# One of eight sums made by a ScalarE copy and an adding transfer instead of VectorE, from the fourth unit on

## The chip, the core and the metric

The kernel runs on one core of a Trainium2 chip. The core has five engines that work beside each other, each in its own program order, and wait for each other through semaphores: TensorE (PE for its products, PEld for loading their weights), VectorE (DVE), ScalarE (ACT), GpSimd (POOL) and SyncE (SP), which only issues transfers. ScalarE and GpSimd can issue transfers too. The metric is the device time of one execution in microseconds (us); lower is better.

## The reference

Two stages. The first is a recurrent attention over 4 batches, 8 heads, 768 positions and 48 columns a head:

```
state = 0                                         # per batch and head, 48 x 48
for t in range(768):
    y[t]  = r[t] @ (state + (u * k[t]) outer v[t])
    state = w[t][:, None] * state + k[t] outer v[t]
```

The second takes y as x, 3072 rows (batch and position) of 384 columns, through two layers, all in float32:

```
h = x @ w_in                    # 384 -> 2048
g = h * (1 / (1 + exp(-h)))
out = g @ w_out                 # 2048 -> 384
```

The change touches what is made of g ahead of the last product.

## The kernel before

The work is cut into 12 units. A unit is 128 positions of two batches, so 256 rows of x; units 0 to 11 go through the batches' halves, then on to the next 128 positions. The first units differ from the rest; from unit 3 on (`NFAST = 3`) everything named below is alike.

**Rounds.** The loop of line 1442 runs over i = 3 to 11. In round i three units are in work: the attention of unit i (the groups that `mix(i)` lists, lines 965 to 1071), the first layer of unit i - 1 (`ups`, 20 steps) and the second layer of unit i - 2 (`downs`, 7 steps). The seven steps of `downs` come first and the 20 of `ups` behind them; the groups are laid between them, each with a count of steps that follow it. After round 11 come the second layer of unit 10, the first layer of unit 11 and the second of unit 11, with no attention beside them: the tail. The order of every engine's program is the order in which these lines are reached; each engine keeps to it, and no planner moves anything.

**First layer.** Each of the 20 steps of `ups` is one `first_part(i, n)`: eight products of 64 columns of weights on TensorE into one of four banks, and then a copy, a sum or the activation that the step owes. The 20 steps stand for the layer's block products; sums of weights and of x take the place of some blocks. The results, g, are eight tiles of 128 partitions by 512 columns, named `gt[i, x, b, m]`: x the lower or upper half of the 2048 columns, b the batch, m which half of that half. Step 17 makes `gt[i, 1, 0, 0]`, step 18 and step 19 make tiles of m = 1.

**Sums for the second layer.** The second layer is computed with seven products of blocks instead of eight (line 1322), and four of these take sums of g's blocks on their left. `sums(i, m)` (line 1293) makes the four for one half m, into `quarters`, a part of the tile `temps`:

```
s1 = lower[1] + upper[1]     s3 = lower[0] - lower[1]
s2 = s1 - lower[0]           s4 = upper[0] - s2
```

in this order, each 128x512, at line 1306 on VectorE. `sums(i, 0)` stands behind step 17, `sums(i, 1)` behind step 19. (Unit 3 makes two of its m = 1 sums a round later.) So eight sums a unit, four for each m.

**Second layer.** The seven products run in the order of `downs`: the first two take g itself, the third s2, the fourth s1, the fifth s3, the sixth s4, the seventh g again. Each takes the eight tiles f of one kind, the four of m = 0 first. They add into three banks in the order x, z, x, y, x, y, x (`place`, line 1326). After the second, fifth and sixth, VectorE adds the bank to a part that ScalarE has copied out (line 1343); after the others ScalarE copies it (line 1340). So the seventh product, which adds to bank x, has to wait until VectorE has read bank x after the fifth.

**What stands around the sums in a round.** Ahead of step 17, VectorE writes into the scores (`block_write`, L573). Behind it GpSimd has `bonus_steps(i + 1, 1, 2, 3)`, four multiplications at L497 (in round 4 step 0 of it and a product as well, in round 5 seven products of `tw` at L414 stand ahead of step 17). Then come steps 18 and 19 and the last group: the attention's output on TensorE, copied by ScalarE (`kq` L831, `yt` L873), VectorE's transposes of the next unit's `tk` (L365), which GpSimd's next work (L655) reads, and the update of the state. The next round starts with the second layer's first products, VectorE's transposes of `tr`, its work on the queries (L628, L783) and on sums of x (L1152 to L1172), among which the L1343 after the fifth product has its fixed place.

**Transfers.** SP issues nearly all: loads of the next units in small pieces, the way of y through device memory to x (`turned<-yt`, `xt<-turned`), the output. ScalarE issues a few in the first units. GpSimd issues none.

## Time and profile before

| | us |
|---|---|
| median of three runs | 566.93 (566.53 to 567.62) |
| the profiled execution | 567.41 |
| its span, first instruction to last | 565.6 |
| busy: TensorE products, weights | 555.8, 517.6 |
| busy: VectorE, GpSimd, ScalarE | 477.0, 395.7, 274.5 |
| VectorE's sums at L1306, 128x512, s1 and s3 of both m | 36 of 0.985 on average |

The profile is that of one execution, 0.48 us above the median of the runs. Lines L... are those of the kernel's file; where several places call one helper, all have its line. An instruction of the timeline shows its start, its length, engine, line, operation, what it writes <- what it reads, shapes, how many were merged into the row, and in brackets the idle time ahead of it with what ended it. GpSimd's spans are rough. The steady rounds take 42.4 us each from the start of one second layer to that of the next (298.68, 341.12, 383.55 in the chain of work that ended last), and the last two 41.1.

### The profile page before, as it was taken

The numbers are of one execution on the slowest core, as the hardware profiler recorded it, in microseconds if no ns is written. First come the engines' busy times: TensorE is split into PE (matmuls) and PEld (weight loads), VectorE is DVE, ScalarE is ACT, GpSimd is POOL, SyncE is SP. The second block draws the span as 40 slices with busy tenths as digits, with TensorE's granted clock in tenths as the row PEclk, the third lists the DMA queues.
The fourth block names the chain that finished last, engine by engine and source line by source line (L and its number), as shares of the span: only waits on it lengthen the run. The fifth ranks groups of instructions, "written<-read, shape, count | busy, mean of one in ns | idle before, by whom it ended". The sixth has DMA issues, their size and how long they took to land.

```text
span 565.6 us, 18886 instructions
## 1 busy us (share of the span) xinstructions
PE 555.8 (98%) x7782; PEld 517.6 (92%) x7782; DVE 477.0 (84%) x744; ACT 274.5 (49%) x620; POOL 395.7 (70%) x447
## 2 busy tenths in 40 slices
PE   8989999999999999999999999999999999999997
PEld 8767786699889999999999999999999999999997
DVE  7979788998999989999889989989989989882250
ACT  5679696362371373373374274274274272371330
POOL 5998988617879998969796696696696696700000
PEclk9999999999999999999999999999999999999999
DMA  9956876345345365365565554555555462102000
GB/s 224 314 104 191 213 213 133 49 69 115 99 76 99 80 105 94 59 131 95 104 104 93 113 93 89 108 96 94 111 88 95 99 102 65 38 5 57 29 9 21
DMA packets 206485, 57.59 MB, mean 102 GB/s; under 512 B 186048, under 2 KB 198208, under 8 KB 206400
## 3 DMA queue, kind: packets, MB, share of 16 engines
q1 hardware_dynamic: 203712, 54.23, 46.9%
q10 hardware_dynamic: 2688, 2.16, 1.6%
q8 instruction: 61, 1.00, 0.8%
q14 instruction: 24, 0.20, 0.1%
HBM read 47.14 MB, written 9.18 MB: 100 GB/s over the span
## 4 chain that ended last, share of the span: by engine, by line
PE 78%; DVE 8%; POOL 7%; DMA 3%; issue 2%; ACT 1%; SPq 0%; POOLq 0%; DVEq 0%
PE p_o L1335 24%; PE p_o L1191 14%; PE p_h L1191 9%; PE p_h L1084 8%; PE p_h L1335 4%; PE p_m L1273 4%; PE p_sc L704 3%; PE p_m L868 2%; PE p_sc L1335 2%; POOL tk L646 2%; POOL w_in_sb L260 2%; PE p_m L847 1%; DVE tr L628 1%; PE p_m L704 1%; POOL tw L414 1%
## 5 line engine op out<-in xcount | busy, mean ns | idle before, releaser
L646 POOL TENSOR_TENSOR tk<-tk,tw 128x256 f32<-128x256 f32 x112 | 91.7, 839 | 7.6 <-DVE tw L414 3.4
L1335 PE MATMUL p_o<-own,temps 128*128 128x192 f32 x496 | 82.9, 326 | 0.0
L1335 PEld LDWEIGHTS p_o<-own,temps 128*128 128x128 f32 x496 | 80.8, 190 | 0.3 <-DVE temps L1306 0.2
L1191 PE MATMUL p_o<-xt,w_in_sb 128*64 128x128 f32 x1152 | 72.5, 273 | 0.1
L414 POOL TENSOR_TENSOR tw<-tw 128x256 f32<-128x256 f32 (+6 forms) x71 | 42.3, 596 | 38.0 <-DVE tw L365 34.5
L1084 PE MATMUL p_h<-xt,w_in_sb 128*128 128x256 f32 x288 | 66.1, 384 | 1.8 <-POOL w_in_sb L260 1.6
L1191 PEld LDWEIGHTS p_o<-xt,w_in_sb 128*64 128x64 f32 x1152 | 64.9, 137 | 0.4 <-issue 0.4
L1084 PEld LDWEIGHTS p_h<-xt,w_in_sb 128*128 128x128 f32 x288 | 53.6, 190 | 10.0 <-POOL w_in_sb L260 2.4
L497 POOL TENSOR_TENSOR ruk<-tokens_rk 128x384 f32<-128x384 f32 x48 | 53.6, 1137 | 8.1 <-DMA tokens_rk<-in_k_dram 8.1
L1335 PE MATMUL p_o<-w_out_sb,gt 128*128 128x192 f32 x308 | 54.5, 330 | 0.4 <-DVE ob L1343 0.3
L628 DVE TENSOR_TENSOR tr<-tr,tw 128x512 f32<-128x512 f32 x57 | 51.9, 911 | 1.0 <-PE p_m L704 0.4
L1335 PEld LDWEIGHTS p_o<-w_out_sb,gt 128*128 128x128 f32 x308 | 50.0, 190 | 1.5 <-DVE ob L1343 0.9
L655 POOL TENSOR_TENSOR tk<-tk,tw 128x256 f32<-128x256 f32 x32 | 25.1, 812 | 27.5 <-DVE tk L365 27.5
L1306 DVE TENSOR_TENSOR temps<-gt 128x512 f32<-128x512 f32 (+1 forms) x48 | 42.9, 931 | 0.0
L1340 ACT COPY partial<-p_o 128x192 f32<-128x192 f32 x31 | 9.9, 319 | 66.6 <-PE p_o L1335 61.5
L616 ACT COPY tk<-tk 128x256 f32<-128x256 f32 x52 | 20.9, 402 | 37.2 <-POOL tk L646 27.4
L1215 ACT ACTIVATE gt<-p_o 128x512 f32<-128x512 f32 x45 | 26.0, 601 | 25.0 <-PE p_o L1191 25.0
L1335 PE MATMUL p_o<-w_out_sb,temps 128*128 128x192 f32 x176 | 30.5, 326 | 0.0
L722 DVE COPY_PREDICATED score<-mask,p_sc 128x512 f32<-128x512 int8 x38 | 28.4, 807 | 1.4 <-PE p_sc L704 1.3
L1335 PE MATMUL p_h<-w_out_sb,gt 128*128 128x192 f32 x168 | 29.1, 326 | 0.0
L1335 PEld LDWEIGHTS p_o<-w_out_sb,temps 128*128 128x128 f32 x176 | 28.9, 190 | 0.1
L497 POOL TENSOR_TENSOR spare<-tokens_rk 128x384 f32<-128x384 f32 x24 | 28.5, 1198 | 0.6
(251 smaller groups left out, 1314.0 us busy)
## 6 DMA issues: line engine op xcount, KB each, us to landing
w_out_sb<-in_moe_w_in_dram SPq DMA_DIRECT2D x6, 768.0 KB, 7.4
turned<-yt SPq DMA_DIRECT2D x18, 192.0 KB, 2.7
xt<-turned SPq DMA_DIRECT2D x9, 384.0 KB, 3.3
w_out_sb<-in_moe_w_out_dram SPq DMA_DIRECT2D x4, 768.0 KB, 7.4
own<-in_moe_w_out_dram SPq DMA_DIRECT2D x4, 768.0 KB, 4.7
tokens_w<-in_w_dram SPq DMA_DIRECT2D x8, 384.0 KB, 4.5
tokens_rk<-in_r_dram SPq DMA_DIRECT2D x7, 384.0 KB, 4.4
tokens_rk<-in_k_dram SPq DMA_DIRECT2D x7, 384.0 KB, 5.8
```

What stands on the lines that cost most here:

```text
L414: engine.tensor_tensor(out=up, in0=t[:, :, 0::2], in1=t[:, :, 1::2], op=ALU.mult)
L497: mul = lambda out, one, two: nc.gpsimd.tensor_tensor(out=out, in0=one, in1=two, op=ALU.mult)
L628: nc.vector.tensor_tensor(out=odd, in0=odd, in1=tw[i][l][:, :, 0::2][:, :, :, None].to_broadcast([128, Q, L >> (l + 1), c]), op=ALU.mult)
L646: nc.gpsimd.tensor_tensor(out=out, in0=have, in1=odd_products(i, l, b, *blocks), op=ALU.mult)
L655: nc.gpsimd.tensor_tensor(out=have, in0=have, in1=odd_products(i, l, b, [2, NP * ni]), op=ALU.mult)
L704: nc.tensor.matmul(to, lhsT=tk[i][rows, X[l % 2] + p, x * 64:(x + 1) * 64], rhs=have, start=True, stop=True)
L722: nc.vector.copy_predicated(out=dst, mask=masks[l][:, :, None].to_broadcast([128, NB, NP, ni, c]), data=sc[e].rearrange("p (b q) (i c) -> ...
L1084: nc.tensor.matmul(p_h[:, a, :], lhsT=w_in_sb[:, c, f * 128:(f + 1) * 128], rhs=xt[i][:, c, :], start=(a == 0 and c == 0), stop=(a == 1 an ...
L1191: nc.tensor.matmul(p[h:h + PD, q, :], lhsT=left[:, f:f + PD], rhs=right, start=first and q == 0, stop=q == 3, skip_group_check=True)
L1215: nc.scalar.activation(out=g(f, t), in_=have, func=AF.Silu)
L1306: nc.vector.tensor_tensor(out=out, in0=one, in1=two, op=op)
L1335: nc.tensor.matmul(p, lhsT=left(f), rhs=right[:, f, :], start=which in (0, 1, 3) and f == 0, stop=f == FH - 1, skip_group_check=True)
```

## The change

From unit 3 on, and for m = 0 alone, s1 is no longer made by VectorE. ScalarE copies `lower[1]` into the place of s1, and a transfer issued by GpSimd adds `upper[1]` to it there (`accum_op`). The other seven sums of a unit stay on VectorE; s2 reads what the transfer leaves. The four sums of m = 0 are also split over two steps: s1 and s3 stay behind step 17, s2 and s4 go behind step 18. In units 1 and 2 nothing changes, and no sum has another value.

```diff
@@ def sums(i, m, which=range(4)):
         made = ((s1, lower[1], upper[1], ALU.add), (s3, lower[0], lower[1], ALU.subtract),
                 (s2, s1, lower[0], ALU.subtract), (s4, upper[0], s2, ALU.subtract))
-        for out, one, two, op in (made[x] for x in which):
-            nc.vector.tensor_tensor(out=out, in0=one, in1=two, op=op)
+        for x in which:
+            out, one, two, op = made[x]
+            if x == 0 and i >= NFAST and m == 0:
+                nc.scalar.copy(out=out, in_=one)
+                nc.gpsimd.dma_start(out=out, in_=two, accum_op=ALU.add)
+            else:
+                nc.vector.tensor_tensor(out=out, in0=one, in1=two, op=op)
@@ def ups(i):
             made = [[(first_part, i, n)] for n in ORDER]
             if i == len(units) - 1:
                 made[10].append((sums_of_x, i, 7))
-            made[17].append((sums, i, 0))
+            made[17].append((sums, i, 0, (0, 1)))
+            made[18].append((sums, i, 0, (2, 3)))
             made[-1].append((sums, i, 1, range(4) if i > NFAST else (0, 2)))
             return made
```

## The prediction

> **What bounds the kernel now.** I read the page's busy shares first, then its forty slices.

> ```profile
> PE 555.8 (98%) x7782; PEld 517.6 (92%) x7782; DVE 477.0 (84%) x744; ACT 274.5 (49%) x620; POOL 395.7 (70%) x447
> ...
> DVE  7979788998999989999889989989989989882250
> ```

> TensorE is busy for 98% of the span, VectorE nearly always until the last four slices, ScalarE half the time. So the change eases an engine that is full but is not the bound: it gains only where TensorE waits for VectorE, and loses wherever VectorE or GpSimd becomes late for TensorE. Next, the list of waits, for what little TensorE waits for:

> ```profile
> PEld p_sc L704 <- POOL tk L646: 2.3, 9, 0.5
> ...
> PEld p_o L1335 <- DVE ob L1343: 0.9, 2, 0.6
> ```

> Total us, times, longest us: small (the next such line, of L1191 behind L1218, has 0.8), but they name the tight places. L1335 behind L1343 is the seventh product of a unit's second layer (I call it Q7; line 1334): it adds to the bank "x" that VectorE's sum after the fifth product must have read. So I read the end of a steady round, round 7, and the start of round 8 in the timeline, engine by engine:

> ```profile
> 336.95 2.89 DVE L1306 TENSOR_TENSOR temps<-gt 128x512 f32<-128x512 f32 x2
> 339.77 1.50 DVE L1306 TENSOR_TENSOR temps<-temps,gt 128x512 f32<-128x512 f32 x1
> 341.37 0.69 DVE L1306 TENSOR_TENSOR temps<-gt,temps 128x512 f32<-128x512 f32 x1
> ...
> 344.51 1.30 DVE L365 STREAM_TRANSPOSE tk<-raw 128x512 f32<-128x512 f32 x2
> ...
> 356.12 0.36 DVE L1343 TENSOR_TENSOR ob<-p_o,partial 128x192 f32<-128x192 f32 x1
> ...
> 334.87 3.00 POOL L497 TENSOR_TENSOR ruk<-ruk,u_bc 128x384 f32<-128x384 f32 x2
> 337.84 1.46 POOL L497 TENSOR_TENSOR spare<-tokens_rk 128x384 f32<-128x384 f32 x1
> 339.37 1.34 POOL L497 TENSOR_TENSOR tokens_rk<-tokens_rk,tokens_w 128x384 f32<-128x384 f32 x1
> 345.30 3.04 POOL L655 TENSOR_TENSOR tk<-tk,tw 128x256 f32<-128x256 f32 x4 [4.58 <-DVE tk L365]
> ...
> 336.36 1.09 ACT L1215 ACTIVATE gt<-p_h 128x512 f32<-128x512 f32 x2
> ...
> 356.59 2.63 PEld L1335 LDWEIGHTS p_o<-w_out_sb,gt 128*128 128x128 f32 x16
> ```

> Columns: start and length in us. Three things to see. VectorE runs without an idle time from the sums of L1306 to the sum of L1343, which ends at 356.48, and Q7's first weights load at 356.59: 0.11 us of slack (the same in rounds 7, 9 and 10; in round 11, 481.76 against 482.55, 0.8). A sum of L1306 takes 0.69 us (every 0.61) while GpSimd is idle, and 1.5 (every 1.42) while GpSimd multiplies at L497; those multiplications, 1.0 each alone, take 1.3 to 1.5. And GpSimd starts these four at 334.87, before the sums.

> **The change, part by part.**

> *Removed:* nine sums s1 on VectorE (units 3 to 11): 1.42 us in a steady round.

> *Added on ScalarE:* nine copies of 128x512. The nearest row is ScalarE's copy of L785, the same shape, 0.61 at 329.53. The copy stands behind the activation that feeds the fourth sum, second of the pair at 336.36, which ends at 337.45; so it ends at 338.0. What is behind it on ScalarE moves by 0.6: two activations, two copies of kq that end at 339.2, then copies of yt that have 0.6 us of idle time ahead of them. The update's products read kq at 340.2. Cost nothing; without that idle time up to 0.6 a round.

> *Added on GpSimd's queue:* the transfer, which must wait for the copy. GpSimd gets there at 334.87, and it works in order, so the four multiplications of L497 wait until 338.0 plus what issuing takes. No row shows a transfer issued by GpSimd. Bounds for the issue: 0 (the engine goes on at once) and 2.0 (two multiplications of L497); I take 1.0, one multiplication. They then run from 339.0. They were followed by 4.6 us of idle time, so GpSimd's own end costs nothing; what counts is that they now meet other sums.

> *Added, issue to landing:* 256 KB within on-chip memory. Rows: 64 KB to `kept` 1.6, 192 KB `turned<-yt` 2.7, 384 KB `xt<-turned` 3.3, 384 KB `tokens_rk<-in_k_dram` 6.9 on ScalarE's queue. I take 3.5, just above the third, since the bytes it adds to are read too; ends 1.6 and 6.9. [...]

> *The new wait:* s2 reads s1, so VectorE stops until 338.0 + 3.5 = 341.5, after finishing s3 near 337. Behind s2 stand s4, the four sums of the other half, the transposes of tk and tr, the queries and x sums of the next round, and L1343. Cost in a steady round: by 341.5 GpSimd has done 2.5 multiplications; 1.5 remain and meet sums. From the landing to the transposes: 1.5 x 1.42 + 4.5 x 0.61 = 4.9, so 346.4 against 344.51: **VectorE is 1.9 late**, although a sum fewer. This hardly depends on my two unknowns: a sooner landing only meets more multiplications. Landing in 1.6 with free issue gives 339.65 + 2.4 x 1.42 + 3.6 x 0.61 = 345.2, 0.7 late. At 6.9 and 2.0: 344.9 + 6 x 0.61 = 348.6, 4.1 late.

> *Where it reaches TensorE:* nothing idles on VectorE until L1343, so Q7 waits 1.9 − 0.11 = 1.8. The products that read the sums do not feel it: the second uses of s2 end near 345.8, and are read from 347.6. The bursts of scores have over 4 us.

> *Moved:* s2 and s4 go one step later in the program, behind the four multiplications (another engine's) and a first-layer step. On VectorE nothing lies between; cost nothing, since the transfer is later anyway.

> *Sum.* Rounds 6 to 9 (paid at Q7 of rounds 7 to 10): 4 x 1.8 = 7.2. Round 10 (paid in 11): 1.9 − 0.8 = 1.1. Two earlier rounds differ:

> ```profile
> 250.17 6.18 POOL L414 TENSOR_TENSOR tw<-tw 128x512 f32<-128x512 f32 x7
> ...
> 259.64 1.29 DVE L365 STREAM_TRANSPOSE tk<-raw 128x512 f32<-128x512 f32 x2
> ```

> Round 4: the activation ends at 209.4, the copy at 210.0, landing 213.5; GpSimd has over seven operations then, so all four sums behind meet them: 213.5 + 4 x 1.42 = 219.2, against transposes at 217.66 in the timeline: 1.5 late; Q7 already waits for VectorE there (0.56), so 1.5 in full. Round 5: seven products hold GpSimd until 256.3, so the transfer starts only then, or from 255 if the quieter VectorE lets them run faster; landing 259.2 on the mean, + 4.9 = 264.1 against 259.64: 4.4 late, and Q7 waits there already (0.38): 4.4. Rounds 11 and the tail: GpSimd is empty; in the tail the copy ends at 543.9, landing 547.4, the second s2 ends at 550.5 and is read from 550.7: nothing.

> Total 7.2 + 1.1 + 1.5 + 4.4 = 14.2. The profiled execution took 567.41 (span 565.6), so 581.6; it lies 0.48 above the median of the runs, 566.93, so **581.1**. Low ends: 4 x 0.6 + 0 for round 11 + 0 for round 4 (all four sums from 211.6 end before 217.66) + 2.6 for round 5 = 5.0: 572. High ends: 4 x 4.0 + 3.3 + 3.3 + 5.9, and 3 in the tail = 31.5: 598.

> **The rivals.**

> *Faster: VectorE is relieved.* Slices of 9 speak for it. Decides if s2 needs no wait, and GpSimd's postponed multiplications fall beside the transposes, not the sums: without them the six sums take 3.7, so the landing must come before 340.8, under 2.8 after the copy. The gain is bounded by TensorE's waits for VectorE after 180 us, 0.9 + 0.8 (L1191 behind L1218), and for GpSimd's tk, which follows VectorE, 1.2 of the 2.3; I take half, 1.5: 565.4. Against it: the multiplications must go somewhere, and even a free landing at 338.0 gives 338.0 + 4 x 1.42 + 2 x 0.61 = 344.9, 0.4 late. [...]

> *No change: the lateness is absorbed.* The chain from the sums to L1343 would have to give back 1.9 us in 12; VectorE shows no idle time there. Needs a Q7 wait that the trace misnames. 567.

> *Worse: the transfer is the slow thing.* An adding transfer of 7 us gives the 598 above, and each further us costs one in eight places (rounds 4 to 10 and the tail): 614 at 9 us. Transfers of small pieces run beside it (DMA share 0.49 from 334 to 345), for it; 256 KB in rows of 2 KB, against.

> **How the numbers follow.** Forecast (VectorE late at Q7) 0.80, for 572 to 592: its ends are 572 and 598, and landings past 6 us are unlikely beside the rows of 2.7 and 3.3; slow transfer 0.07; faster 0.08; no change 0.05. The range 572 to 592 leaves out the other three, 0.2. Within 0.2% is 1.1 us either way, about what runs of this kernel can tell apart: faster 0.08, same 0.05, slower 0.87.

> **What would show it.** Right: idle time on VectorE ahead of L1306 in every unit from the fourth, ended by a transfer; L497 starting about 4 us later in its round; PEld L1335 waiting for L1343 some 14 us in all, most in round 6. Wrong: L1343 no later against Q7, sums of 0.69 throughout, or TensorE waiting at L1335 for the sums themselves.

## The result, and the profile after

The changed kernel takes 586.67 us (median; 585.5 to 590.31) against 567.27 of the kernel before: 1.0354 times as long, 95% interval 1.0335 to 1.0374. The forecast was 581.1 us in a range of 572 to 592, slower with a chance of 0.87. The profiled execution took 587.73 us (span 585.7), 20.3 more than that of before. In the new file the copy is line 1308, the transfer 1309, VectorE's sums 1311, the second layer's products 1340, ScalarE's copies of its banks 1345 and VectorE's sums of them 1348.

From the page of the changed kernel: busy shares, the granted clock in forty slices, the chain's shares by engine, and two groups (busy us, mean ns; then idle us ahead of them and what ended most of it).

```profile
PE 560.7 (96%) x7782; PEld 519.8 (89%) x7782; DVE 458.2 (78%) x735; ACT 279.0 (48%) x629; POOL 390.6 (67%) x456
...
PEclk9999999999999999999899999999999999999999
...
PE 57%; DVE 18%; issue 11%; DMA 5%; SPq 3%; POOL 3%; ACT 3%; DVEq 0%; POOLq 0%
...
L1311 DVE TENSOR_TENSOR temps<-temps,gt 128x512 f32<-128x512 f32 (+1 forms) x25 | 21.9, 877 | 46.2 <-DMA temps<-gt 46.1
...
L1309 POOL DMA_DIRECT2D temps<-gt x9 | 8.0, 886 | 63.5 <-ACT temps L1308 60.7
```

VectorE is busy 18.8 us less than before (477.0), more than the 9 × 1.42 = 12.8 of the sums taken away: those left are shorter too, and so are the writes into the scores (L573, 24.0 us against 27.0), as they meet fewer of GpSimd's multiplications (in round 7 the second of them took 1.92 us beside L497 before, and 1.33 with GpSimd idle now). But it stands still for 46 us behind the transfer, which was not there before, and TensorE fell from 98% of the span to 96%. Its 7782 products are the same; that they take 4.9 us more, and the slice whose clock reads 8, is the first sign (TensorE's granted clock in these traces is 1.0, full, or 0.5, half; the slice is a mean of both) of something that the prediction had no term for.

The waits of the changed kernel (total us, times, longest us) say where that standing still arrives, and the list of transfers gives the median from issue to landing:

```profile
DVE temps L1311 <- DMA temps<-gt: 46.1, 9, 6.4
PEld p_o L1340 <- DVE ob L1348: 14.9, 7, 3.5
...
```

```profile
temps<-gt POOLq DMA_DIRECT2D x9, 256.0 KB, 4.0
```

TensorE's wait at the seventh product of the second layer (Q7) has grown from 0.9 us to 14.9. The steady round that the prediction worked through, round 7, now looks like this in the timeline of the changed kernel, engine by engine (start, length in us; in brackets the idle time before and what ended it):

```profile
346.70 0.68 DVE L1311 TENSOR_TENSOR temps<-gt 128x512 f32<-128x512 f32 x1
353.78 0.69 DVE L1311 TENSOR_TENSOR temps<-temps,gt 128x512 f32<-128x512 f32 x1 [6.41 <-DMA temps<-gt]
...
357.72 1.30 DVE L365 STREAM_TRANSPOSE tk<-raw 128x512 f32<-128x512 f32 x2
...
348.58 0.87 POOL L1309 DMA_DIRECT2D temps<-gt  x1 [3.33 <-ACT temps L1308]
349.18 2.28 POOL L497 TENSOR_TENSOR ruk<-ruk,u_bc 128x384 f32<-128x384 f32 x2
...
352.49 1.01 POOL L497 TENSOR_TENSOR tokens_rk<-tokens_rk,tokens_w 128x384 f32<-128x384 f32 x1
...
347.67 0.62 ACT L1308 COPY temps<-gt 128x512 f32<-128x512 f32 x1
...
369.71 1.44 PEld L1340 LDWEIGHTS p_o<-w_out_sb,gt 128*128 128x128 f32 x9 [2.76 <-DVE ob L1348]
```

Up to here the changed kernel has lost 10.33 us (351.38 against 341.05 at the start of the next second layer), so subtract that to compare with the times in the prediction. Read from the top: VectorE makes s3 and then has nothing for 6.41 us; ScalarE's copy ends at 348.29; GpSimd, idle for 3.33 us, issues 0.3 us later; the data lands at 353.76, 5.17 us after the issue began. By then GpSimd has done its four multiplications (353.50), so the six sums run unhindered (353.78 to 357.72). The transposes start at 357.72 − 10.33 = 347.39 in the time of before, against 344.51: 2.9 us late, and Q7 waits 2.76.

What each round lost, from the starts of the second layers of the two profiled executions (worked out, start after minus start before, less the same of the round before):

| lost in round | 5 | 6 | 7 | 8 | 9 | 10 | 11 | tail |
|---|---|---|---|---|---|---|---|---|
| forecast, us | 1.5 | 4.4 | 1.8 | 1.8 | 1.8 | 1.8 | 1.1 | 0 |
| measured, us | 2.39 | 6.52 | 1.86 | 2.73 | 2.30 | 2.29 | 1.61 | 0.87 |

The tail is counted to the end of the span; up to the start of the last second layer it lost nothing. Together these are 20.6; the spans differ by 20.1, as the changed kernel was 0.43 us ahead where this count begins.

### The profile page after: what moved, and what is told of

It reads as the page before. It is cut to its first block, busy times and chain, and to the rows that moved or that the text cites. A ratio compares the mean times of both kernels' runs of the same rounds, so it can differ in the third digit from the quotient of the medians.

```text
span 585.7 us, 18908 instructions
## 1 busy us (share of the span) xinstructions
PE 560.7 (96%) x7782; PEld 519.8 (89%) x7782; DVE 458.2 (78%) x735; ACT 279.0 (48%) x629; POOL 390.6 (67%) x456
## 4 chain that ended last, share of the span: by engine, by line
PE 57%; DVE 18%; issue 11%; DMA 5%; SPq 3%; POOL 3%; ACT 3%; DVEq 0%; POOLq 0%
PE p_o L1340 13%; PE p_o L1191 11%; PE p_h L1084 8%; PE p_h L1191 8%; PE p_m L1273 4%; DVE tr L628 3%; SPq L127 3%; PE p_sc L704 3%; DVE temps L1311 2%; DVE block_sums L534 2%; DMA temps<-gt 2%; DVE score L722 2%; PE p_m L868 1%; PE p_m L847 1%; PE p_m L704 1%
## 5 line engine op out<-in xcount | busy, mean ns | idle before, releaser
L646 POOL TENSOR_TENSOR tk<-tk,tw 128x256 f32<-128x256 f32 x112 | 92.2, 843 | 8.0 <-DVE tw L414 3.8
L1191 PE MATMUL p_o<-xt,w_in_sb 128*64 128x128 f32 x1152 | 72.1, 273 | 0.0
L1340 PE MATMUL p_o<-w_out_sb,gt 128*128 128x192 f32 x308 | 57.6, 342 | 12.8 <-DVE ob L1348 12.8
L414 POOL TENSOR_TENSOR tw<-tw 128x256 f32<-128x256 f32 (+6 forms) x71 | 40.8, 574 | 40.9 <-DVE tw L365 37.4
L1340 PEld LDWEIGHTS p_o<-w_out_sb,gt 128*128 128x128 f32 x308 | 52.2, 197 | 15.5 <-DVE ob L1348 14.9
L1191 PEld LDWEIGHTS p_o<-xt,w_in_sb 128*64 128x64 f32 x1152 | 64.7, 137 | 0.1
L497 POOL TENSOR_TENSOR ruk<-tokens_rk 128x384 f32<-128x384 f32 x48 | 52.9, 1131 | 7.9 <-DMA tokens_rk<-in_k_dram 7.9
L1311 DVE TENSOR_TENSOR temps<-temps,gt 128x512 f32<-128x512 f32 (+1 forms) x25 | 21.9, 877 | 46.2 <-DMA temps<-gt 46.1
L1309 POOL DMA_DIRECT2D temps<-gt x9 | 8.0, 886 | 63.5 <-ACT temps L1308 60.7
L616 ACT COPY tk<-tk 128x256 f32<-128x256 f32 x52 | 20.9, 402 | 59.8 <-POOL tk L646 39.7
L655 POOL TENSOR_TENSOR tk<-tk,tw 128x256 f32<-128x256 f32 x32 | 24.6, 800 | 31.7 <-DVE tk L365 31.7
L1345 ACT COPY partial<-p_o 128x192 f32<-128x192 f32 x31 | 9.9, 318 | 59.9 <-PE p_o L1340 59.8
L1215 ACT ACTIVATE gt<-p_o 128x512 f32<-128x512 f32 x45 | 25.9, 601 | 24.7 <-PE p_o L1191 24.7
```

Source lines behind the costliest of these rows:

```text
L414: engine.tensor_tensor(out=up, in0=t[:, :, 0::2], in1=t[:, :, 1::2], op=ALU.mult)
L497: mul = lambda out, one, two: nc.gpsimd.tensor_tensor(out=out, in0=one, in1=two, op=ALU.mult)
L646: nc.gpsimd.tensor_tensor(out=out, in0=have, in1=odd_products(i, l, b, *blocks), op=ALU.mult)
L655: nc.gpsimd.tensor_tensor(out=have, in0=have, in1=odd_products(i, l, b, [2, NP * ni]), op=ALU.mult)
L1191: nc.tensor.matmul(p[h:h + PD, q, :], lhsT=left[:, f:f + PD], rhs=right, start=first and q == 0, stop=q == 3, skip_group_check=True)
L1215: nc.scalar.activation(out=g(f, t), in_=have, func=AF.Silu)
```

## The experiments

The theory: VectorE takes its work in order, so it is late by whatever the transfer's landing makes it late, and TensorE pays at the place without slack, Q7. GpSimd, in order too, is held until the copy ends, so its multiplications fall on VectorE's later sums. The rivals were other places for the cost: the split of the steps, the landing alone, the meetings alone, the issue on GpSimd. Runs of one group share runs of the kernel before: 566.96 us for the first four, 567.13 for the last four.

### The split alone

```
 for x in which:
     out, one, two, op = made[x]
-    if x == 0 and i >= NFAST and m == 0:
-        nc.scalar.copy(out=out, in_=one)
-        nc.gpsimd.dma_start(out=out, in_=two, accum_op=ALU.add)
-    else:
-        nc.vector.tensor_tensor(out=out, in0=one, in1=two, op=op)
+    nc.vector.tensor_tensor(out=out, in0=one, in1=two, op=op)
```

> The copy and the transfer are undone: s1 is VectorE's again in every unit. Only the split stays (s1 and s3 behind step 17, s2 and s4 behind step 18). Theory (the cost is VectorE's wait for the transfer): VectorE's order is unchanged, so 567 us within 1, and the seventh product waits for VectorE as before (0.9 us in all). Rival (placing s2 and s4 a step later costs by itself): 570 or more.

Measured: 567.27 us, ratio 1.0005 (0.9996 to 1.0015). The move of s2 and s4 by a step costs nothing that can be measured; the whole loss lies in the copy and the transfer.

### The copy kept, an add on GpSimd in place of the transfer

```
 nc.scalar.copy(out=out, in_=one)
-nc.gpsimd.dma_start(out=out, in_=two, accum_op=ALU.add)
+nc.gpsimd.tensor_tensor(out=out, in0=out, in1=two, op=op)
```

> ScalarE's copy stays; instead of the transfer GpSimd adds upper[1] in place with one 128x512 sum, in the same place of its queue. Theory A (what I predicted: GpSimd held behind the copy, and its four multiplications then meeting VectorE's sums): the sum is there 1.6 us after the copy, but s2 and the three sums behind it take 1.42 each, so VectorE is 2.0 late in rounds 6 to 10, 4.9 in round 5, and the time is 580 to 584. Theory B (the landing alone is the cost, meetings cost little): s2 is no later than before in rounds 6 to 10, 1.6 late in round 5: 568 to 570.

Measured: 581.72 us, ratio 1.0258 (1.0243 to 1.0273). Rounds 7 to 10 lose 1.65 or 1.66 each. The timeline of this kernel in a steady round, VectorE and then GpSimd:

```profile
303.55 1.48 DVE L1311 TENSOR_TENSOR temps<-temps,gt 128x512 f32<-128x512 f32 x1 [2.32 <-POOL temps L1309]
305.13 1.30 DVE L1311 TENSOR_TENSOR temps<-gt,temps 128x512 f32<-128x512 f32 x1
306.36 2.91 DVE L1311 TENSOR_TENSOR temps<-gt 128x512 f32<-128x512 f32 x2
...
310.51 1.30 DVE L365 STREAM_TRANSPOSE tk<-raw 128x512 f32<-128x512 f32 x2
```

```profile
302.25 1.27 POOL L1309 TENSOR_TENSOR temps<-temps,gt 128x512 f32<-128x512 f32 x1 [3.12 <-ACT temps L1308]
303.48 2.41 POOL L497 TENSOR_TENSOR ruk<-ruk,u_bc 128x384 f32<-128x384 f32 x2
```

Here s1 is ready 1.27 us after the copy, far sooner than any transfer, and the loss stays three quarters of the whole: four sums meet four multiplications. From 303.55 to 310.51 are 6.96 us, which is 4 × 1.42 + 2 × 0.61 = 6.9. So the two causes stand in for each other: an earlier landing buys meetings, as the prediction had it. The copy's end is what both hang on.

### The same copy and transfer, earlier

Both inputs of s1 are there some steps before. Here the copy and the transfer stand behind step 15 of the unit instead of step 17.

```
+if i >= NFAST and tuple(which) == (0,):        # the whole step: copy, then transfer
+    s1 = quarters[:, 0, 4 * m:4 * m + 4, :]
+    nc.scalar.copy(out=s1, in_=gt[i, 0, 1, m][:, :, :])
+    nc.gpsimd.dma_start(out=s1, in_=gt[i, 1, 1, m][:, :, :], accum_op=ALU.add)
+    return
...
-made[17].append((sums, i, 0, (0, 1)))
+made[15].append((sums, i, 0, (0,)))
+made[17].append((sums, i, 0, (1,)))
```

> Copy and transfer are issued behind step 15, as soon as lower[1] exists, two steps earlier. Both theories have the transfer issued near 335.2 of a steady round instead of 338.4 and landed by 339.2, when VectorE took up s2 in the kernel before (339.8). Theory (the wait for the landing is the cost, and an earlier place takes it away): 567 to 569, no wait of VectorE for the transfer over 2.5 us, the seventh product's wait for VectorE under 3 us in all. Rival (the copy on ScalarE or the transfer beside others costs wherever it stands): 573 or more.

Measured: 567.54 us, ratio 1.0005 (0.9983 to 1.0027). From the waits of this kernel, and its timeline in the round of before's 336.95:

```profile
DVE temps L1317 <- DMA temps<-gt: 13.0, 9, 3.1
...
PEld p_o L1346 <- DVE ob L1354: 0.9, 3, 0.4
```

```profile
338.10 0.69 DVE L1317 TENSOR_TENSOR temps<-temps,gt 128x512 f32<-128x512 f32 x1 [0.74 <-DMA temps<-gt]
...
343.49 1.30 DVE L365 STREAM_TRANSPOSE tk<-raw 128x512 f32<-128x512 f32 x2
...
334.67 0.87 POOL L1298 DMA_DIRECT2D temps<-gt  x1 [0.22 <-issue]
335.27 2.95 POOL L497 TENSOR_TENSOR ruk<-ruk,u_bc 128x384 f32<-128x384 f32 x2
```

GpSimd waits 0.22 us instead of 3.33 and VectorE 0.74 instead of 6.41; Q7 is back at 0.9 in all. One part of the expectation was missed: the longest wait of VectorE for the transfer is 3.1 us, not under 2.5, at 297.81, behind a transfer that took 5.75; TensorE did not feel it. The whole loss in the rounds is gone with the operations unchanged, so it was the place, not the price, of the copy and the transfer. And nothing is gained: VectorE starts its transposes 0.6 us earlier than before (343.49 against 344.51, in an execution that ran 0.46 us ahead at this place), and no place of TensorE can use it. That answers the first rival of the prediction: relief for VectorE, when it does come, is worth nothing measurable here.

### Unit 4 left on VectorE

```
-if x == 0 and i >= NFAST and m == 0:
+if x == 0 and i >= NFAST and i != 4 and m == 0:
```

> The change for all units from 3 on but unit 4, whose transfer is held up behind seven products on GpSimd and pays in round 6. Round 6 took 6.5 us longer in the changed kernel: 3.5 of wait at the seventh product, 1.3 at the third, and some 2.5 in which the granted clock of TensorE stood at 0.5 behind that wait. Theory (the clock falls because TensorE stood still there for 3.5 us): all 6.5 go, 580 to 581.5, the granted clock stays at 1.0. Rival (the clock falls for another reason, such as the new transfers as a whole): only 4 go, 582.5 to 584, and a stretch of 0.5 shows up elsewhere.

Measured: 581.95 us, ratio 1.0273 (1.0248 to 1.0298). Round 6 lost 0.12 instead of 6.52, so that round's loss was unit 4's transfer. But round 8 lost 4.10 instead of 2.73, in a stretch of TensorE at half clock (3.41 us from 363.04) that round 8 of the changed kernel had not shown. So the time fell between the two ranges expected, above the 581.5 of the theory: the round's loss went, as the theory had it, and half clock turned up elsewhere, as the rival had it. The rival's reason, the new transfers as a whole, is not needed for that: why half clock came there is told below, with the clock.

### The other half's sums first

s2 and s4 of the first half moved behind the four sums of the second, so that the landing has something to hide behind.

```
-made[18].append((sums, i, 0, (2, 3)))
 made[-1].append((sums, i, 1, range(4) if i > NFAST else (0, 2)))
+made[-1].append((sums, i, 0, (2, 3)))
```

> Copy and transfer as in the changed kernel; s2 and s4 of m = 0 go behind the four sums of m = 1 in VectorE's order, so that these run while the transfer is on its way. If waiting for the landing is the whole cost, the transfer is covered in rounds 6 to 10 and only round 5 (transfer held behind seven products) stays late: 568 to 570. If the postponed multiplications of GpSimd cost wherever they meet sums (theory), the four sums of m = 1 meet them from 339: 339.0 + 4 x 1.42 + 2 x 0.61 = 345.9, 1.4 late in each of rounds 6 to 10, 2.5 in round 5, nothing in round 4: 573 to 576.

Measured: 582.26 us, ratio 1.0263 (1.0244 to 1.0283). Both numbers missed: the steady rounds still lose 1.97 to 2.00 each, though VectorE now waits for the transfer in one unit of nine only, 0.8 us. From the timeline of this kernel, VectorE and GpSimd:

```profile
344.49 5.07 DVE L1311 TENSOR_TENSOR temps<-gt 128x512 f32<-128x512 f32 x2 [1.96 <-ACT gt L1215]
349.49 0.68 DVE L1311 TENSOR_TENSOR temps<-temps,gt 128x512 f32<-128x512 f32 x1
...
352.14 1.30 DVE L365 STREAM_TRANSPOSE tk<-raw 128x512 f32<-128x512 f32 x2
```

```profile
343.77 0.88 POOL L1309 DMA_DIRECT2D temps<-gt  x1 [3.34 <-ACT temps L1308]
344.37 2.27 POOL L497 TENSOR_TENSOR ruk<-ruk,u_bc 128x384 f32<-128x384 f32 x2
346.30 1.29 POOL L497 TENSOR_TENSOR spare<-tokens_rk 128x384 f32<-128x384 f32 x1
```

Two things took the landing's place. The second half's sums wait 1.96 us for ScalarE's activations, 0.6 of which is the copy ahead of them. And the first of those sums lasts 3.65 us (344.49 to 348.14; 0.69 alone), while GpSimd's first three multiplications run at 1.3 each beside it; the second takes 1.49. So VectorE lost the landing's wait and paid with another wait and a harder meeting. I had priced each meeting at 1.42, the measure of rows in which sums and multiplications alternate; here a sum arrived at a run of multiplications under way, and that price was too low. In each of the seven units 3 to 9 one sum lasted 3.65 to 5.70 us.

### The transfer behind the four multiplications

GpSimd's multiplications first, as before the change, and the transfer issued after them.

```
+if i >= NFAST and m == 0 and tuple(which) == (2, 3):
+    nc.gpsimd.dma_start(out=quarters[:, 0, 0:4, :], in_=gt[i, 1, 1, 0][:, :, :], accum_op=ALU.add)
...
 nc.scalar.copy(out=out, in_=one)
-nc.gpsimd.dma_start(out=out, in_=two, accum_op=ALU.add)
```

> The transfer is issued behind GpSimd's four multiplications instead of ahead of them, so these stay where they were in the kernel before and meet no other sums; the transfer starts near 340.8 of a steady round and lands 4 later, at 344.8. Theory (landing first, then six sums at 0.61): VectorE 3.9 late in rounds 6 to 10, 5 in round 4, 10 in round 5, 33 in all, and each wait of TensorE over 2.5 may bring a stretch at half clock of 3.4 (1.7 lost) behind it: 600 to 614. Rival (GpSimd being held is what costs): less than the changed kernel, under 587.

Measured: 611.76 us, ratio 1.0784 (1.0763 to 1.0805); rounds 6 to 10 lose 6.4 to 9.1 each. With no sums met and a later landing the loss more than doubles: a landing behind the multiplications saves no meeting any more, and half clock comes on top. In the waits of this kernel two places pay, and the first never more than 3.5 at a time:

```profile
PEld p_o L1342 <- DVE ob L1350: 19.1, 7, 3.5
PEld p_o L1342 <- DVE temps L1313: 8.0, 7, 1.3
...
PEld p_o L1342 <- issue: 5.8, 2, 3.0
```

The last two are at the third product, which reads the sums themselves (the 5.8, put down to nothing, are its waits in rounds 5 and 6, at 220.27 and 268.60). Together 32.9 us, of a loss of 43.9 at the second layers. The clock was at half speed in five stretches of 3.41 or 6.83 us, 23.9 in all; half of that by estimate, 12, is about the 11 that are left.

### The changed kernel with TensorE kept busy in round 6

Twelve transposes of the identity, whose result nothing uses, ahead of Q7 in round 6: the kernel computes the same and does a little more.

```
-return [[(quarter, i, x)] for x in range(7)]
+return [[*([(beat, 6), (beat, 6)] if (i, x) == (4, 6) else []), (quarter, i, x)] for x in range(7)]
```

> The changed kernel with twelve 128x128 transposes of the identity (2.8 us of work without a use) on TensorE ahead of the seventh product in round 6, inside its wait of 3.5 us. Theory (the clock of 0.5 behind that wait is due to TensorE standing still): no stretch of 0.5 there, round 6 takes 2 to 3 us less than in the changed kernel, 584 to 585. Rival (the clock falls for another reason): the stretch stays, 586.5 to 588.

Measured: 586.4 us, ratio 1.0339 (1.0323 to 1.0355), above the 584 to 585 expected. The transposes took 1.47 us there, not 2.8. Round 6 lost 3.80 instead of 6.52 and stayed at full clock, with Q7 starting when VectorE was done as before: 2.7 of its 6.5 us were the clock. But in this execution round 10 was struck, at half clock for 3.41 us from 457.56, and lost 4.29 instead of 2.29, so the total did not move. That the transposes are what kept round 6 at full clock is not shown; the section on the clock tells why.

### The sum on GpSimd, without copy and transfer

```
-nc.scalar.copy(out=out, in_=one)
-nc.gpsimd.dma_start(out=out, in_=two, accum_op=ALU.add)
+nc.gpsimd.tensor_tensor(out=out, in0=one, in1=two, op=op)
```

> s1 of m = 0 made by GpSimd in one sum, without a copy on ScalarE and without a transfer, in the place where the changed kernel issues the transfer. Nothing holds GpSimd there in a steady round: s1 runs from 334.9 to 336.2, the multiplications 1.3 later than before. Theory: no loss in rounds 6 to 10 (VectorE a sum shorter, four sums meet multiplications: 336.4 + 0.6 + 4 x 1.42 + 0.61 = 343.3, ahead of 344.5), nothing gained either, since TensorE is full; in round 5 GpSimd reaches it only at 256.3, behind seven products, VectorE 4.9 late, and round 6 takes 4.5 longer: 571 to 574. Rival (any work moved onto GpSimd costs in every round): 576 or more.

Measured: 573.01 us, ratio 1.0098 (1.008 to 1.0116). The steady rounds lose 0.2 each, round 6 loses 5.45 (GpSimd comes to the sum behind its seven products of L414; VectorE waits 3.50 for it there, Q7 3.52, then 3.41 us at half clock). Without the copy, GpSimd is not held, and its own add costs the steady rounds next to nothing, where an add behind a copy cost 1.66: that difference is the copy with the hold behind it. It is 1% slower than the kernel before, clear of noise; no version here is faster than that kernel.

### The clock, from all the traces together

Stretches of half clock came at one wait and not at another as long. In every trace they begin at multiples of 3.413 us from each other: in the kernel with the late transfer 47.78, 51.20, 47.79 and 51.20 us apart (14, 15, 14, 15 times 3.413), in the changed kernel 310.61 (91 times) from that of 276.39 to the next, at 587.00, behind the last instruction. I call this a grid. I therefore cut each trace at its own grid and read TensorE's busy time window by window. Of the changed kernel (window; length, busy us and instructions of PE, PEld, DVE, ACT, POOL; granted clock; DMA share, GB/s), and of the copy with the add on GpSimd:

```profile
272.97:276.39 3.42, 1.35 (x9) 1.05 (x7) 3.40 (x8) 1.02 (x2) 3.26 (x5) 1.00 0.40 49
276.39:279.80 3.41, 2.26 (x7) 2.26 (x8) 3.33 (x7) 0.00 (x0) 3.33 (x5) 0.50 0.41 50
279.80:283.21 3.41, 3.41 (x19) 2.97 (x21) 1.97 (x3) 0.15 (x1) 2.66 (x3) 0.50 0.18 60
...
457.29:460.71 3.42, 1.54 (x9) 1.54 (x10) 3.32 (x7) 0.00 (x0) 3.26 (x5) 1.00 0.42 51
```

```profile
225.88:229.29 3.41, 1.12 (x7) 1.12 (x8) 3.13 (x6) 0.62 (x2) 3.41 (x4) 1.00 0.41 51
229.29:232.71 3.42, 3.42 (x12) 3.42 (x11) 2.53 (x4) 0.92 (x2) 3.34 (x5) 0.50 0.31 42
273.67:277.08 3.41, 1.53 (x10) 1.24 (x8) 3.41 (x10) 1.02 (x2) 3.25 (x5) 1.00 0.41 49
277.08:280.50 3.42, 2.08 (x13) 2.08 (x14) 3.32 (x8) 0.00 (x0) 3.34 (x5) 1.00 0.41 52
```

The windows with 1.35 and 1.12 us of TensorE work were followed by one at half clock, those with 1.53 and 1.54 were not. Past 60 us and up to the tail, this holds for every window of the nine traces of the changed kernel and its variants: ten windows at full clock had 0.18 to 1.35 us of work and all ten were followed by half clock; all others had 1.50 or more and none was. TensorE's busy time alone does not tell them all apart, though: near 35 us, in three of the nine traces (the split alone, unit 4 left on VectorE, the other half first), a window with 1.82 to 1.86 us was followed by half clock too. About 1.0 of that was small products of 48x64; whether these count for less is open. Half clock ended after the first window in which TensorE worked all of its 3.41 us; after windows of 2.26 and 2.57 it went on for another. So long waits that fell into one window were struck, and one that a boundary cut was spared: the 3.52 us in the copy-and-add kernel's round 6 were cut (1.53 and 2.08 us of work on either side), the 2.63 us in round 10 of the kernel with the transposes and the 2.45 us in round 8 of the kernel that leaves unit 4 on VectorE were not. The grid lay differently against the program in each execution (its first boundary at 0.13 to 3.32 us), so which of the long waits is struck may change from run to run. This explains a part of the spread of the changed kernel's times at most: the slowest run (590.31) had a mean granted clock of 0.990, the other three 0.994. By these means it was at half clock some 4.7 us longer, worth about 2.4 us by estimate, of the 2.6 to 4.8 by which it is behind them; and the run of 587.73 had the same 0.994 as that of 585.5.

The kernel with the transposes has to be read again with this. Of that kernel (round 6, then round 10), and of the one that leaves unit 4 on VectorE (round 8):

```profile
273.25:276.66 3.41, 3.07 (x23) 2.81 (x22) 3.41 (x10) 1.02 (x2) 3.33 (x4) 1.00 0.39 48
276.66:280.07 3.41, 1.81 (x11) 1.81 (x12) 3.31 (x7) 0.00 (x0) 3.25 (x5) 1.00 0.40 52
454.15:457.56 3.41, 1.07 (x7) 0.78 (x6) 3.31 (x7) 0.00 (x0) 3.33 (x5) 1.00 0.41 49
```

```profile
359.63:363.04 3.41, 1.26 (x8) 0.96 (x7) 3.31 (x8) 0.00 (x0) 3.26 (x5) 1.00 0.42 53
```

In round 6 a boundary cut the long wait. All the transposes lay in the first of the two windows, which without their 1.47 us would still have had 1.60, and the second had 1.81 without any. Windows with as much work (1.50 us or more) were not struck in any of these traces past 60 us. So this execution shows what round 6 costs at full clock, and does not test whether keeping TensorE busy prevents half clock.

## Why the prediction was right, point by point

**The bound, and "relieving VectorE gains only where TensorE waits".** Right, and shown from both sides: slower when VectorE is late, and no gain when it is early (the early transfer, 1.0005).

**Removed, and "moved: cost nothing".** Right: the split alone, 1.0005.

**The copy on ScalarE, "cost nothing else".** Right for the steady rounds: it took 0.62 (forecast 0.61), ended at 348.29, which is 337.96 in the time of before (forecast 338.0), and the idle time ahead of the copies of yt took it up (350.13 against 339.79 + 10.33 = 350.12). It did cost where I moved the other half's sums ahead: there the 0.6 was part of VectorE's wait.

**Issue on GpSimd, 1.0.** Measured 0.87 (1.00 in the first unit). What the prediction left out was the way from ScalarE's end to GpSimd's start, 0.3 us. GpSimd's multiplications started at 349.18 − 10.33 = 338.85, forecast 339.0.

**Issue to landing, 3.5 (1.6 to 6.9).** Too low: 3.93, 4.04, 3.44, 5.17, 4.13, 4.18, 3.99, 4.12 and 3.30 us, median 4.0, of which the last, with nothing beside it in the tail, is the shortest. The value was taken from rows of transfers that do not add, issued by SP or ScalarE; what made this one longer, the adding, GpSimd's queue or the traffic beside it, no run separates.

**VectorE 1.9 late, Q7 waits 1.8 in each steady round.** The mechanism was right, the size short: 1.86, 2.73, 2.30 and 2.29, together 9.2 against 7.2. The term that was mis-sized is the landing. In these rounds it came 3.44 to 5.17 us after the issue and 0.3 for the handing over, 1.0 later on the mean than 338.0 + 3.5; half of that was given back, since fewer sums met a multiplication (in round 7 none did). The sentence that the lateness "hardly depends on my two unknowns" is true of an early landing, as the copy with the add showed (1.66 with s1 ready after 1.27 us), and not of a late one, as the late transfer did: past the end of the multiplications nothing is given back. The prediction's own ends, 0.7 and 4.1 late, already spoke against that sentence.

**Round 11 (1.1) and the tail (0).** Round 11 lost 1.61: right but for the same landing. The tail lost 0.87. The third product of the last second layer waits for the sums there:

```profile
570.22 1.27 PEld L1340 LDWEIGHTS p_sc<-own,temps 128*128 128x128 f32 x8 [0.37 <-DVE temps L1311]
```

The other 0.5 lies behind the last output's landing: from there to the end of the span it is 1.55 us, against 1.03 before. So it is in all six kernels in which GpSimd issues transfers, the early one too, and in none of the four others; the prediction had no term for it.

**Round 4, paid in 5: 1.5 at Q7.** It lost 2.39, and not at Q7, whose wait stayed at 0.56. The timeline of the changed kernel:

```profile
219.71 6.47 PEld L1340 LDWEIGHTS p_o<-own,temps 128*128 128x128 f32 x40 [1.25 <-DVE temps L1311]
227.40 2.57 PEld L1340 LDWEIGHTS p_o<-w_out_sb,temps 128*128 128x128 f32 x16 [1.21 <-ACT partial L1345]
230.53 2.57 PEld L1340 LDWEIGHTS p_o<-w_out_sb,gt 128*128 128x128 f32 x16 [0.56 <-DVE ob L1348]
```

Two steps failed. "The products that read the sums do not feel it" was worked out in the steady round and carried over; here the third product waits 1.25 for them. And the sixth waits 1.21 for a copy of ScalarE (L1345) that stands behind a copy of tk (L616), which waits for GpSimd's tk (L655), which waits for VectorE's transposes: VectorE's lateness, 2.35 us here (219.58 + 0.43 against 217.66), came round through two other engines that I had left out.

**Round 5, paid in 6: 4.4.** The waits were near it: Q7 3.52 against 0.38 before, and 0.69 at the third product, 3.8 in all; the rest of the 6.52 is the term that was missing, TensorE's clock at one half for 6.83 us from 276.39. Where that stretch did not come, in the kernel with the transposes, the round lost 2.7 less, and 3.8 + 2.7 is 6.5.

**The sum.** 14.2 forecast; 20.6 by the table. Steady rounds +2.0, the clock in round 6 +2.7 with the waits there 0.6 less, round 5 +0.9, round 11 +0.5, the tail +0.9: 6.4. That 586.67 lies within the range is partly luck: its upper part was meant for later landings, and 2.7 us of it were filled by a clock that the prediction put at nothing.

**The signs.** VectorE's idle time in every unit and the later multiplications came as described. So did "some 14 us in all" at Q7 (14.9, of which 0.9 was there before), but by errors that cancel: the steady rounds waited 2.1 more there than forecast and round 11 0.4, rounds 5 and 6 1.5 and 1.3 less. Round 6 had the longest of these waits (3.52), not most of them. And one sign of being wrong did show: TensorE waited for the sums themselves, 1.25 us in round 5, 0.69 in round 6 and 0.37 in the tail.

**The rivals.** *Faster:* needed the landing under 2.8 us after the copy; the nearest was 3.6 (3.30 + 0.3), and the early transfer shows the gain would have been nothing. Moving a sum off VectorE gained nothing here, where VectorE was busy for 84% of the span and TensorE for 98%. *No change:* Q7 waits 14.9 us. *Slow transfer:* landings stayed under 5.2. Its price was put too low: in the late transfer s1 is there at 366.46 − 21.05 = 345.4 in the time of before, near the 344.9 of my high end, and its rounds 7 to 10 lose 6.4 to 7.7 each, not 4.0, since the waits at the third product (1.1 to 1.3) and the clock come on top of those at Q7 (3.5).

## What to carry to other kernels

In this kernel an engine that is nearly full but is not the bound earned nothing when relieved, and cost the bound whatever made it late, at the next place without slack; look for that place, and for the ways round through other engines, before moving its work. A copy and an adding transfer belong where their inputs are ready and their reader is 4 to 6 us away (the landings came 3.3 to 5.75 us after the issue), and the engine that issues the transfer should have nothing urgent behind it: here the same two instructions, two steps earlier, cost nothing. When TensorE is the bound, price a wait like those of 2.45 to 3.52 us struck here twice, once for itself and once for the half clock that may follow (1.4 to 2.7 us here).
